# Agent attention with a squared-ReLU layer on one core: TensorE matmuls split over pairs of 64-row tiles

## The chip, the core and the metric

One core of one Trainium2 chip. The metric is the device time in microseconds from the start to the end of one execution. Five engines work side by side and meet at semaphores: TensorE (PE: matmuls and weight loads), VectorE (DVE), ScalarE (ACT), GpSimd (POOL) and SyncE (SP, which issues the DMAs). TensorE writes its results to PSUM, eight banks of 512 fp32 columns on 128 partitions; ACT and DVE read them there.

## The reference

Agent attention over 4 batches of 12480 tokens with 128 channels and 49 agents, and behind it a two-layer network of width 2048 with relu(h)² between its layers, on all 49920 tokens:

```python
s1 = scale * (agents @ k.T);  a2k = softmax(s1);  agent_v = a2k @ v     # 49 x 128
s2 = scale * (q @ agents.T);  q2a = softmax(s2);  x = q2a @ agent_v     # tokens x 128
h = x @ w_in;  r = maximum(h, 0);  g = r * r;  out = g @ w_out          # 128 -> 2048 -> 128
```

All in fp32. The softmax adds 1e-9 to its sum.

## The kernel before, in words

**Folding.** `x @ w_in` is `q2a @ (agent_v @ w_in)`, so for each batch the kernel makes W = agent_v @ w_in (49 x 2048) and multiplies the 49 probabilities of a token straight into it. Where two operands go into a matmul each is split in a high part, rounded to fp32r, and the low rest, and three products are summed: high·high, high·low, low·high.

**Blocks.** The tokens go in 52 groups s of 960 (ST), two halves of 480 columns (TT) side by side in two PSUM banks. The 2048 hidden units go in 16 pieces of 128. A block i = 16 s + j is one group and one hidden piece; there are 832 of them, and each goes through this chain:

- `mm1` (L371): h = the three products of W and the probabilities, into a pair of banks. It is called for two blocks at once. The 49 high rows, the 49 low rows and 28 of the 49 rows of the third product are stacked on 126 partitions, so that one matmul of 126 rows (L381, tiles w_a and p_a) does most of it; the other 21 rows sit in four copies at partitions 0, 32, 64 and 96 (w_b, p_b), and four matmuls of 21 rows, one for each half of each of the two blocks, go into four different row groups of the array (L384).
- `relu` on ACT (L388), `square` on ACT (L392), `high` on DVE (L396, gh: the rounded part), `low` on DVE (L400, gl = g − gh).
- `mm2` (L402, matmuls at L411): out += wo_hi·gh + wo_lo·gh + wo_hi·gl, six matmuls of 128 rows and 480 columns, accumulated over the 16 blocks of a group in two banks (out0, out1); then `store` (L425) copies one half with ACT, the other with DVE, and SP writes them out.

The step numbers set the order of each engine: a list of (time, function) pairs is sorted and issued in that order. At step i stand mm1(i), mm1(i+1) and their relus (even i), square, high and low of block i, and mm2 of block i − LAG, with LAG = 4. In this order low(i) stands directly behind high(i) on DVE, and needs its result.

**Attention beside it.** `plan_tokens` places for each later group: `q_scores` (L318: eight fp32 matmuls, which the trace shows as 16 passes, 49 columns moving and 120 columns of weights), a softmax over DVE, ACT and POOL, the split into high and low, eight transposes (L355), copies into p_a, and `q_spread`, five DMAs that put the rows at their partitions. `plan_batch` places for each next batch 13 tiles of keys (`k_scores`, L159) in the first half of a batch's time, and 13 tiles of values (`v_acc`, L213, added up by `v_sum`, L220, on DVE) in its second half, then four `w_make` (L295 to L301), whose low rows reach w_a and w_b by DMA. `chain` gives each operation the first free step of its engine, and counts the attention's two PSUM banks (pool ps_a); `hop` says how many steps must lie between engines. PSUM holds two pairs for h, two banks for out, two for attention. The first batch's attention runs ahead of the blocks.

## Time and profile before

| | before |
|---|---|
| median of 3 runs | 2051.46 us (2050.95 to 2055.99) |
| span of the profiled execution (its own time is given by this span alone) | 2049.0 us |
| what the median has above that span | 2.5 us |
| PE busy, weight loads busy | 2023.5 us, 1585.0 us |
| DVE, ACT, POOL busy | 1832.5, 1728.7, 245.7 us |
| granted TensorE clock, mean | 0.995 |

The span runs from the first to the last instruction of the execution. PE and PEld are the matmuls and the weight loads of TensorE, which run beside each other. A matmul's end is modelled, so its duration (about 380 ns for 480 columns) is longer than the time from its start to the next one's start, and this second time is what a matmul costs in a row of them. In a timeline, equal instructions that follow on one another are drawn together, with their count behind the x; square brackets give idle time of the engine and what ended it. Names are those of the program: p_a is the tile of probabilities, w_a and w_b those of W, gh and gl the two parts of g, ps_att a bank of the attention.

### The profile page before, as it was taken

The numbers are of one execution on the slowest core, as the hardware profiler recorded it, in microseconds if no ns is written. First come the engines' busy times: TensorE is split into PE (matmuls) and PEld (weight loads), VectorE is DVE, ScalarE is ACT, GpSimd is POOL, SyncE is SP. The second block draws the span as 40 slices with busy tenths as digits, with TensorE's granted clock in tenths as the row PEclk, the third lists the DMA queues.
The fourth block names the chain that finished last, engine by engine and source line by source line (L and its number), as shares of the span: only waits on it lengthen the run. The fifth ranks groups of instructions, "written<-read, shape, count | busy, mean of one in ns | idle before, by whom it ended". The sixth has DMA issues, their size and how long they took to land.

```text
span 2049.0 us, 30335 instructions
## 1 busy us (share of the span) xinstructions
PE 2023.5 (99%) x11015; PEld 1585.0 (77%) x11019; DVE 1832.5 (89%) x2282; ACT 1728.7 (84%) x2167; POOL 245.7 (12%) x206
## 2 busy tenths in 40 slices
PE   8899999999999999999999999999999999999999
PEld 7677877777778877777777887777777777777777
DVE  6778889999888889999998888999998898989898
ACT  2478789899888888999888888999888888989897
POOL 2100012221000001232100000122210000000000
PEclk9899999999999999999999999999999999999999
DMA  9322122221111122122112121122111111001110
GB/s 294 105 64 69 55 63 69 67 60 40 54 66 60 58 70 69 53 75 59 35 46 78 51 77 59 54 74 69 44 35 51 44 31 45 30 27 44 31 35 25
DMA packets 44425, 124.75 MB, mean 61 GB/s; under 512 B 6292, under 2 KB 15780, under 8 KB 44276
## 3 DMA queue, kind: packets, MB, share of 16 engines
q1 hardware_dynamic: 44178, 122.78, 19.8%
q8 instruction: 86, 1.41, 0.3%
q14 instruction: 63, 0.52, 0.1%
q10 hardware_dynamic: 98, 0.04, 0.0%
HBM read 80.97 MB, written 25.56 MB: 52 GB/s over the span
## 4 chain that ended last, share of the span: by engine, by line
PE 81%; DVE 11%; issue 6%; ACT 2%; DMA 0%; SPq 0%; POOL 0%; DVEq 0%; ACTq 0%
PE out L411 48%; PE h L381 15%; PE h L384 7%; DVE gh L396 4%; PE ps_att L159 3%; PE ps_att L318 3%; DVE gl L400 2%; DVE vs L206 1%; PE ps_att L355 1%; PE ps_att L213 1%; PE out L231 1%; PE ps_att L295 1%; ACT g L392 1%; ACT r L388 0%; PE h L159 0%
## 5 line engine op out<-in xcount | busy, mean ns | idle before, releaser
L400 DVE TENSOR_TENSOR gl<-g,gh 128x960 fp32r<-128x960 f32 x832 | 1015.5, 1221 | 30.6
L388 ACT ACTIVATE r<-h 128x960 f32<-128x960 f32 x832 | 764.0, 974 | 181.1 <-PE h L384 178.3
L392 ACT ACTIVATE g<-r 128x960 f32<-128x960 f32 x832 | 825.7, 1016 | 5.8 <-DVE gl L400 5.8
L411 PE MATMUL out<-gh,wo_hi 128*128 128x480 f32 x1664 | 688.9, 414 | 6.9 <-DVE ob L429 4.1
L396 DVE CAST gh<-g 128x960 fp32r<-128x960 f32 x832 | 585.2, 703 | 92.1 <-ACT g L392 88.7
L411 PE MATMUL out<-gl,wo_hi 128*128 128x480 f32 x1664 | 634.1, 381 | 1.7 <-DVE gl L400 1.2
L411 PE MATMUL out<-gh,wo_lo 128*128 128x480 f32 x1664 | 515.0, 380 | 1.1 <-POOL wo_lo L120 1.1
L381 PE MATMUL h<-p_a,w_a 126*128 126x480 f32 x1664 | 435.8, 383 | 5.5 <-DMA w_a<-w_lo 3.8
L411 PEld LDWEIGHTS out<-gh,wo_hi 128*128 128x128 f32 x1664 | 313.0, 188 | 141.8 <-issue 72.8
L381 PEld LDWEIGHTS h<-p_a,w_a 126*128 126x128 f32 x1664 | 309.9, 189 | 56.0 <-issue 5.6
L411 PEld LDWEIGHTS out<-gh,wo_lo 128*128 128x128 f32 x1664 | 312.9, 188 | 49.2 <-POOL wo_lo L120 1.5
L411 PEld LDWEIGHTS out<-gl,wo_hi 128*128 128x128 f32 x1664 | 314.4, 189 | 42.0 <-DVE gl L400 6.1
L341 POOL TENSOR_TENSOR e<-e,sm 120x392 f32<-120x392 f32 x52 | 55.3, 1063 | 1261.3 <-DVE sm L338 1136.7
L384 PE MATMUL h<-p_b,w_b 21*128 21x480 f32 x1664 | 204.4, 479 | 0.0
L384 PEld LDWEIGHTS h<-p_b,w_b 21*128 21x128 f32 x1664 | 80.2, 181 | 139.4 <-issue 138.5
L318 PEld LDWEIGHTS ps_att<-ag_sb,qt 128*120 128x120 f32 x832 | 96.8, 187 | 3.9 <-issue 0.4
L318 PE MATMUL ps_att<-ag_sb,qt 128*120 128x49 f32 x832 | 94.3, 267 | 0.0
L195 POOL TENSOR_TENSOR pe<-sk,pe 120x392 fp32r<-120x392 f32 x39 | 53.3, 1366 | 234.7 <-ACT pe L192 192.6
L159 PEld LDWEIGHTS ps_att<-ag_sb,kt 128*120 128x120 f32 x688 | 78.6, 185 | 3.0 <-issue 0.5
L159 PE MATMUL ps_att<-ag_sb,kt 128*120 128x49 f32 x688 | 76.7, 264 | 0.1
L348 POOL TENSOR_TENSOR pp<-e,pp 120x392 fp32r<-120x392 f32 x52 | 56.9, 1095 | 156.7 <-ACT pp L345 156.7
L163 ACT COPY sk<-ps_att 120x392 f32<-120x392 f32 x43 | 20.9, 487 | 59.7 <-PE ps_att L159 59.7
(107 smaller groups left out, 966.6 us busy)
## 6 DMA issues: line engine op xcount, KB each, us to landing
kt<-kT SPq DMA_DIRECT2D x52, 480.0 KB
vt<-v SPq DMA_DIRECT2D x52, 480.0 KB
qt<-qT SPq DMA_DIRECT2D x52, 480.0 KB
outT<-ob SPq DMA_DIRECT2D x51, 480.0 KB
p_b<-p_a SPq DMA_DIRECT2D x208, 39.4 KB
p_a<-p_a SPq DMA_DIRECT2D x52, 105.0 KB
raw<-w_in SPq DMA_DIRECT2D x4, 512.0 KB
raw<-w_out SPq DMA_DIRECT2D x4, 512.0 KB
```

What stands on the lines that cost most here:

```text
L159: nc.tensor.matmul(ps[:CH, c * A:(c + 1) * A], kt[:, c, :], ag_sb[:, b, :], start=True, stop=True)
L195: eng.tensor_tensor(out=pes[n][:, :, A:], in0=piece(n), in1=pes[n][:, :, :A].bitcast(F32), op=ALU.subtract)
L318: nc.tensor.matmul(ps[:CH, c * A:(c + 1) * A], qt[:, c * CH:(c + 1) * CH], ag_sb[:, s // NS, :], start=True, stop=True)
L341: eng.tensor_tensor(out=es[s], in0=es[s], in1=sms.pop(s).to_broadcast([CH, G, A]), op=ALU.mult)
L348: eng.tensor_tensor(out=pps[s][:, :, A:], in0=es.pop(s), in1=pps[s][:, :, :A].bitcast(F32), op=ALU.subtract)
L381: nc.tensor.matmul(hs[x][:, t, :TT], wa[:K, (x % NF) * P:(x % NF + 1) * P], pa[:K, t, :], start=True, stop=False)
L384: nc.tensor.matmul(hs[i + r // 2][:, r % 2, :TT], wb[rows, i % NF // 2, :], pb[rows], start=False, stop=True)
L388: nc.scalar.activation(rs_[i], hs.pop(i)[:, :, :TT], AF.Relu)
L392: nc.scalar.activation(gs[i], rs_.pop(i), AF.Square)
L396: nc.vector.tensor_copy(ghs[i], gs[i])
L400: nc.vector.tensor_tensor(out=gls[i], in0=gs.pop(i), in1=ghs[i].bitcast(F32), op=ALU.subtract)
L411: nc.tensor.matmul(o[t][:, :TT], w[:, j, :], x[:, t, :], start=st, stop=sp)
```

## The change

**TensorE.** Nearly all matmuls of the loop are cut into two of 64 partitions (LOW, 0 to 63, and HIGH, 64 to 127), issued in turn, one on each half of the array's rows, each writing its own PSUM bank. `mm1` is called for one block at a time and does three products for each of the two column halves: half 0 on the low tile, half 1 on the high tile, 49 rows each, six matmuls. The four 21-row matmuls are gone. `mm2` has 12 matmuls of 64 rows: in its first half (x = 0) the low tile sums into one output bank and the high tile into the other, in its second half (x = 1) they change banks. Scores, value sums and transposes are cut in the same way. `w_make` (128 rows), and the transposes of `k_max` and `a_final`, stay on the whole array; W's low rows are now written straight from PSUM into w_b by DVE, without a DMA, and `q_spread` has two DMAs where it had five.

**Banks that change tiles.** Before a bank is written by the other tile, `pass_on` puts a `nop` on GpSimd that depends on the last matmul of the first half, and `take_over` makes the first matmul of the second half depend on that nop. Between the two halves of mm2 stands `mm1` of block i. In the block behind the end of a group (`late`), mm1 comes first, and the second half of the next group's scores (`q_half(s, 1)`) stands between.

**ACT and DVE.** square(i) is placed at step i + 1.2, high(i) at i + 1.35, low(i) at i + 2.4; output is five blocks behind (LAG 5). `v_sum` adds two banks where it added one. Two tiles of keys are scored as a pair and copied and reduced by one operation each. The attention has one pair of banks.

On PE, in the middle of the loop. Before, one call of mm1 for two blocks (L381, L384) and mm2 of one block (L411); out_8198 and out_8199 are the two output banks:

```order
L381 MATMUL h<-p_a,w_a 128x480 [waits Activation_49]
L381 MATMUL h<-p_a,w_a 128x480
L381 MATMUL h<-p_a,w_a 128x480 [waits Activation_49]
L381 MATMUL h<-p_a,w_a 128x480
L384 MATMUL h<-p_b,w_b 128x480 x4
L411 MATMUL out_8198<-gh,wo_hi 128x480 [waits DVE_49]
L411 MATMUL out_8198<-gl,wo_hi 128x480 [waits DVE_49]
L411 MATMUL out_8199<-gh,wo_hi 128x480
L411 MATMUL out_8199<-gl,wo_hi 128x480
L411 MATMUL out_8198<-gh,wo_lo 128x480
L411 MATMUL out_8199<-gh,wo_lo 128x480
```

After, the first half of mm2 (L492), mm1 of one block (L464), and the start of mm2's second half:

```order
L492 MATMUL out_6581<-gh,wo_hi 128x480
L492 MATMUL out_6582<-gh,wo_hi 128x480
L492 MATMUL out_6581<-gh,wo_lo 128x480
L492 MATMUL out_6582<-gh,wo_lo 128x480
L492 MATMUL out_6581<-gl,wo_hi 128x480 [waits DVE_49]
L492 MATMUL out_6582<-gl,wo_hi 128x480
L464 MATMUL h<-p_a,w_a 128x480 [waits Activation_49]
L464 MATMUL h<-p_a,w_a 128x480
L464 MATMUL h<-p_b,w_a 128x480 x2
L464 MATMUL h<-p_a,w_b 128x480 x2
L492 MATMUL out_6582<-gh,wo_hi 128x480 [waits Pool_sequencer_49]
L492 MATMUL out_6581<-gh,wo_hi 128x480
```

A block had 2 matmuls of L381, two of L384 and six of L411; it has 6 of L464 and 12 of L492, and the two output banks change places behind mm1.

On DVE, in the middle of the loop; the numbers tell the buffers apart. Before, each gl takes the gh made just ahead of it:

```order
L396 CAST gh_5527<-g_5525 128x960
L400 TENSOR_TENSOR gl_5535<-g_5525,gh_5527 128x960
L396 CAST gh_5540<-g_5538 128x960
L400 TENSOR_TENSOR gl_5542<-g_5538,gh_5540 128x960
L396 CAST gh_5566<-g_5564 128x960
```

After:

```order
L476 CAST gh_7210<-g_7208 128x960
L480 TENSOR_TENSOR gl_7212<-g_7175,gh_7177 128x960
L476 CAST gh_7238<-g_7236 128x960
L480 TENSOR_TENSOR gl_7240<-g_7208,gh_7210 128x960
L476 CAST gh_7266<-g_7264 128x960
```

The two operations still alternate, but gl_7240 takes gh_7210, which was made two instructions earlier.

The diff, cut to its core:

```diff
+    def pass_on(key, mm):
+        relays[key] = nc.gpsimd.nop()
+        tc.add_manual_dep(relays[key].ins, mm.ins.name, SYNC, reason="bank changes row tile")
+
+    def take_over(key, mm):
+        if key in relays:
+            tc.add_manual_dep(mm.ins, relays.pop(key).ins.name, SYNC, reason="bank changes row tile")
...
     def v_acc(n):
...
         for c in range(G):
-            nc.tensor.matmul(pss["v", n][:A2, :VW], pe[:, c, :], vs[:, c], start=c == 0, stop=c == G - 1)
+            for t, rows in enumerate((LOW, slice(64, CH))):
+                nc.tensor.matmul(ps[:A2, t, :VW], pe[rows, c, :], vs[rows, c], start=c == 0, stop=c == G - 1)
...
     def q_spread(s):
         pa, pb = PT[s]
-        nc.sync.dma_start(out=pa[A2:K].bitcast(F32), in_=pa[:X].bitcast(F32))
-        for r in range(4):
-            nc.sync.dma_start(out=pb[32 * r:32 * r + R].bitcast(F32), in_=pa[X:A, r % 2].bitcast(F32))
+        nc.sync.dma_start(out=pb[:A].bitcast(F32), in_=pa[64:M, 0].bitcast(F32))
+        nc.sync.dma_start(out=pb[64:M].bitcast(F32), in_=pa[:A, 1].bitcast(F32))
...
     def mm1(i):
...
-        for x in (i, i + 1):
-            hs[x] = ps_h.tile([P, 2, 512], F32, name="h")
+        hs[i] = new_h()
+        for n in range(3):
             for t in range(2):
-                nc.tensor.matmul(hs[x][:, t, :TT], wa[:K, (x % NF) * P:(x % NF + 1) * P], pa[:K, t, :], start=True, stop=False)
-        for r in range(4):
-            rows = slice(32 * r, 32 * r + R)
-            nc.tensor.matmul(hs[i + r // 2][:, r % 2, :TT], wb[rows, i % NF // 2, :], pb[rows], start=False, stop=True)
+                rows = slice(64 * t, 64 * t + A)
+                w, p = (wb if n == 2 else wa)[rows, f], pb[rows] if n == 1 else pa[rows, t, :]
+                nc.tensor.matmul(hs[i][:, t, :TT], w, p, start=n == 0, stop=n == 2)
...
+    def mm2(i, x):
...
+        for n, (w, g) in enumerate(((wo_hi, gh), (wo_lo, gh), (wo_hi, gl))):
+            for t, rows in enumerate((LOW, HIGH)):
+                u = t ^ x ^ (j % 2)
+                mm = nc.tensor.matmul(o[u][:, :TT], w[rows, j, :], g[rows, u, :], start=j == 0 and x == 0 and n == 0, stop=j == NF - 1 and x == 1 and n == 2)
+                take_over(("o", i), mm)
+        if x == 0:
+            pass_on(("o", i), mm)
...
-    LAG = 4
+    LAG = 5
...
-    hop = {"PE": {"PE": 1, "ACT": 0, "DVE": 0}, "ACT": {"PE": 2, "ACT": 1, "DVE": 0, "POOL": 0, "SP": 0},
+    hop = {"PE": {"PE": 1, "ACT": 0, "DVE": 0}, "ACT": {"PE": 2, "ACT": 1, "DVE": 0, "POOL": 3},
...
     for i in range(NG + LAG):
+        j, late = i - LAG, i < LAG or (i - LAG) % NF == 0
         if i < NG:
-            if i % 2 == 0:
-                at(i, mm1, i)
-                at(i + .1, relu, i)
-                at(i + .12, relu, i + 1)
-            at(i + .55, square, i)
-            at(i + .6, high, i)
-            at(i + (.65 if i % 2 else 1.25), low, i)
+            at(i if late else i + .01, mm1, i)
+            at(i + .1, relu, i)
+            at(i + 1.2, square, i)
+            at(i + 1.35, high, i)
+            at(i + 2.4, low, i)
...
+        if j >= 0:
+            at(i + (.01 if late else 0), mm2, j, 0)
+            at(i + .03, mm2, j, 1)
```

More of the change, by code (lines that the diff above doesn't have):

```diff
@@ L290, in w_make @@
         if f == 0 and step == 0:
-            W[b] = (wk.tile([P, F], F32R, name="w_a"), wk.tile([P, NF // 2, P], F32R, name="w_b"))
+            W[b] = (wk.tile([P, F], F32R, name="w_a"), wk.tile([P, F], F32R, name="w_b"))
         wa, wb = W[b]
@@ L350, in q_transpose @@
     def q_transpose(s):
-        PT[s] = (wk.tile([P, 2, TT], F32R, name="p_a"), wk.tile([P, TT], F32R, name="p_b"))
-        for half in range(2):
-            ps = pss["t", s, half] = bank()
-            for c in range(H):
-                nc.tensor.matmul(ps[:A2, c * CH:(c + 1) * CH], pps[s][:, half * H + c, :], ident_r[:CH, :CH], start=True, stop=True)
-    def q_copy(s, half):
-        nc.scalar.copy(PT[s][0][:A2, half, :], pss.pop(("t", s, half))[:A2, :TT])
+        ps = pss["t", s] = new_h() if many[0] else att()
@@ new lines, in q_transpose, with q_copy @@
+        for c in range(G):
+            for t, rows in enumerate((LOW, slice(64, CH))):
+                n = rows.stop - rows.start
+                nc.tensor.matmul(ps[:M, t, c * n:(c + 1) * n], pps[s % 2][rows, c, :], ident_r[rows, rows], start=True, stop=True)
+    def q_copy(s):
+        PT[s] = (wk.tile([P, 2, TT], F32R, name="p_a"), wk.tile([P, TT], F32R, name="p_b"))
+        ps = pss.pop(("t", s))
+        to = PT[s][0][:M].rearrange("p t (c n) -> p (t c) n", n=CH)
+        nc.scalar.copy(to[:, :, :64], ps[:M, 0, :].rearrange("p (c n) -> p c n", n=64))
+        nc.scalar.copy(to[:, :, 64:], ps[:M, 1, :G * (CH - 64)].rearrange("p (c n) -> p c n", n=CH - 64))
@@ L470, in chain @@
                 held = range(ts[0], ts[-1] + 2) if todo[0][0] == "PE" else ()
-                if all(banks.get(y, 0) + need <= 2 for y in held):
+                if not any(y in banks for y in held):
                     break
                 t += 1
-            for y in held:
-                banks[y] = banks.get(y, 0) + need
+            banks.update(held)
             for (e, f, *args), g in zip(todo, ts):
@@ L481, in chain, with plan_queries, plan_queries_early, plan_turns @@
         return first, t
-    reads_bank = (k_copy, k_pmax, k_max, v_sum, a_final, w_make, q_max, q_sub, q_copy)
-    def plan_tokens(s, base, loaded=False):
-        first, end = chain(base, [("PE", q_scores, s), ("DVE", q_max, s), ("DVE", q_sub, s), ("ACT", q_exp, s), ("DVE", q_sum, s), ("DVE", q_inverse, s),
-                                ("POOL", q_norm, s), ("ACT", q_hi, s), ("POOL", q_lo, s),
-                                ("PE", q_transpose, s), ("ACT", q_copy, s, 0), ("ACT", q_copy, s, 1)])
+    reads_bank = (kp_copy, kp_max, k_max, v_sum, a_final, w_make, q_shift, q_copy)
+    def plan_queries(s):
+        t = (s - 3) * NF + NF - 1 + LAG
+        g = t + 1
+        while ("DVE", g) in taken:
+            g += 1
+        banks.update(range(t, g + 2))
+        taken.add(("DVE", g))
+        at(t - 6, q_load, s)
+        at(t + .5, q_half, s, 0)
+        at(t + 1.02, q_half, s, 1)
+        at(g + .5, q_shift, s)
+        _, ends[s] = chain(g + 1, [("ACT", q_exp, s), ("DVE", q_total, s), ("POOL", q_norm, s), ("ACT", q_hi, s), ("POOL", q_lo, s)])
+    def plan_queries_early(s, base, loaded):
+        first, ends[s] = chain(base, [("PE", q_half, s, 0), ("PE", q_half, s, 1), ("DVE", q_shift, s), ("ACT", q_exp, s), ("DVE", q_total, s),
+                                      ("POOL", q_norm, s), ("ACT", q_hi, s), ("POOL", q_lo, s)])
         if not loaded:
             at(first - 6, q_load, s)
+    ends = {}
+    def plan_turns(s):
+        _, end = chain(max(ends[s] + 1, (s - 1) * NF), [("PE", q_transpose, s), ("ACT", q_copy, s)])
         at(end + .9, q_spread, s)
@@ L607, in agent_attention_relu2_kernel @@
     at(3.95, warm_up, 2)
-    plan_tokens(1, 1, True)
+    plan_queries_early(1, 0, True)
+    plan_turns(1)
     for f in range(2, F // 512):
-        _, e = chain(4 * f - 7, [("PE", w_make, 0, f, 0), ("ACT", w_make, 0, f, 1), ("DVE", w_make, 0, f, 2)])
-        at(e + .9, w_make, 0, f, 3)
-    chain(8, [("DVE", wo_make, 3, x) for x in range(7)] + [("ACT", wo_split, 3, 0), ("POOL", wo_split, 3, 1)])
+        chain(4 * f - 7, [("PE", w_make, 0, f, 0), ("ACT", w_make, 0, f, 1), ("DVE", w_make, 0, f, 2)])
+    _, end = chain(8, [("DVE", wo_make, 3, x) for x in range(7)] + [("ACT", wo_split, 3, 0)])
+    at(end + .6, wo_split, 3, 1)
+    assert end < 3 * PW // P + LAG
+    plan_queries_early(2, 9, False)
+    for s in range(3, NSG):
+        plan_queries(s)
     for s in range(2, NSG):
-        plan_tokens(s, (s - 1) * NF)
+        plan_turns(s)
     for b in range(1, B):
```

197 lines of the change are left out of this document (120 added, 77 removed).

## The prediction

> **What bounds the kernel now.** I read the page's busy times first, then the same by stage, then the chain of work that ended last in one stretch of the loop, then single instructions there.
>
> ```profile
> PE 2023.5 (99%) x11015; PEld 1585.0 (77%) x11019; DVE 1832.5 (89%) x2282; ACT 1728.7 (84%) x2167; POOL 245.7 (12%) x206
> PE 81%; DVE 11%; issue 6%; ACT 2%; DMA 0%; SPq 0%; POOL 0%; DVEq 0%; ACTq 0%
> ...
> 300.00:500.00 200.00, 197.29 (x1061) 153.60 (x1061) 196.79 (x236) 184.54 (x246) 49.72 (x37) 1.00 0.21 59
> 500.00:820.00 320.00, 320.00 (x1762) 251.79 (x1760) 276.68 (x347) 269.66 (x331) 21.63 (x19) 1.00 0.20 61
> ```
>
> The columns of the last two rows are window, length, then PE, PEld, DVE, ACT, POOL, clock. TensorE is the bound; at 500 to 820 us it has no gap and DVE has 14% to spare. At 300 to 500 us, where a batch's values are summed (two more stages are like it, 820 to 1000 and 1300 to 1500, 580 us together), DVE is as full as PE, at 98.4%. The clock is full, so PE's time is a count of instructions. The chain shows what one pair of blocks costs:
>
> ```profile
> 613.89 0.86 PE h L381 x4
> 614.76 0.42 PE h L384 x4
> 615.17 2.81 PE out L411 x12
> 617.98 1.62 PE ps_att L159 x16
> ```
>
> Two blocks take 0.86 + 0.42 + 2.81 = 4.09 us; a score tile pushed in takes 1.62. Inside this (timeline of PE and its weight loads; start, duration):
>
> ```profile
> 599.68 0.38 PE L381 MATMUL h<-p_a,w_a 126*128 126x480 f32 x1
> 599.99 0.19 PEld L384 LDWEIGHTS h<-p_b,w_b 21*128 21x128 f32 x4 [0.34 <-issue]
> 599.99 0.49 PE L384 MATMUL h<-p_b,w_b 21*128 21x480 f32 x4
> 600.41 0.19 PEld L411 LDWEIGHTS out<-gh,wo_hi 128*128 128x128 f32 x1 [0.22 <-issue]
> 600.41 0.48 PE L411 MATMUL out<-gh,wo_hi 128*128 128x480 f32 x1
> 600.52 0.19 PEld L411 LDWEIGHTS out<-gl,wo_hi 128*128 128x128 f32 x1
> 600.73 0.37 PE L411 MATMUL out<-gl,wo_hi 128*128 128x480 f32 x1
> 600.73 0.19 PEld L411 LDWEIGHTS out<-gh,wo_hi 128*128 128x128 f32 x1
> 600.94 0.38 PE L411 MATMUL out<-gh,wo_hi 128*128 128x480 f32 x1
> 601.17 0.38 PE L411 MATMUL out<-gl,wo_hi 128*128 128x480 f32 x1
> ```
>
> From start to start a matmul of 480 columns costs .73, .94, .17: 0.21 to 0.23, and L381 0.86/4 = 0.215. I take a slot of 0.2175 us. The next load runs in that time (600.73, beside the matmul of 600.73). At L384 this stops: it starts 0.31 after the matmul ahead of it, the next matmul 0.42 later, and the second after it 0.32 later, 1.05 us for what would be three slots (0.65). Changing from 128-row matmuls to 21-row ones and back costs 0.40 us for each two blocks. The four loads of L384, on four row groups, lie inside 0.19 us, the length of one: separate row groups load and multiply at the same time.
>
> **The change, part by part.**
>
> *The blocks on PE.* A block gets 3 + 6 = 9 pairs of 64-row matmuls, all in one form of the array, so the 0.40 goes; a pair counts as one slot, because row groups run side by side. Two blocks: 18 x 0.2175 = 3.915 us against 4.09, a saving of 0.175; times 416: **−73 us**. The slot of a pair is the one price the trace doesn't show. Below: the four L384 matmuls took 0.42, less one load of 0.11 (600.41 to 600.52) and less the 0.11 by which such a change outlasts a 0.20 stream (0.31 at 599.68), so a stream alone is 0.20. Above: if the two loads of a pair are taken one behind the other, 0.11 + 0.11 = 0.22; if a load isn't hidden at all, 0.20 + 0.11 = 0.31. I take the middle, 0.2175, because the loads in order and the whole array give nearly the same; each 0.001 us of slot is 7488 x 0.001 = 7.5 us of span.
>
> [...]
>
> *The attention on PE.* Rows of the chain:
>
> ```profile
> 306.02 0.67 PE ps_att L355 x8
> ...
> 330.42 0.96 PE ps_att L213 x8
> ```
>
> Transposes: eight pairs with weights of 113 columns where 98 took 0.67, so 0.77: +0.10 x 52 = **+5**. Scores: as many passes on each tile as before, loads side by side: 1.62 stays, but two halves have a boundary more, about 0.1 x 70 = **+7**. Value sums: between nothing (0.96 stays) and loads one behind the other (0.67/8 = 0.084 each, 16 x 0.084 = 1.34): 0 to 15 us over 39 tiles; I take **+5**. The matmuls left on the whole array, six a batch (four of w_make, one transpose each of k_max and a_final), in three batches, now each change the array's form and back: 18 x 0.40 = **+7**.
>
> Each score tile has twice as many instructions, 32 matmul passes. [...] No row here shows a long run of pairs; the shortest sustained step is the 0.084 above.
>
> *The hand-over by GpSimd.* A matmul's modelled end is 0.38 after its start. How long engines take to hear of each other:
>
> ```profile
> 601.83 1.78 PE L159 MATMUL ps_att<-ag_sb,kt 128*120 128x49 f32 x16
> 603.64 0.49 ACT L163 COPY sk<-ps_att 120x392 f32<-120x392 f32 x1 [1.24 <-PE ps_att L159]
> ...
> 562.87 0.20 DVE L338 RECIPROCAL sm<-sm 120x8 f32<-120x8 f32 x1
> 563.21 1.09 POOL L341 TENSOR_TENSOR e<-e,sm 120x392 f32<-120x392 f32 x1 [33.40 <-DVE sm L338]
> ```
>
> PE to ACT 0.03 (603.61 to 603.64), DVE to POOL 0.14. With T the start of the last matmul in mm2's first half, the second half may start its load at T + 4 x 0.2175 − 0.11 = T + 0.76 without loss. The relay needs 0.38 and two hand-overs of 0.03 to 0.14: T + 0.44 to T + 0.66. I take **0**; mm1's three pairs hide it. Without them, up to 0.66 − 0.11 = 0.55 us a block would show. What is queued behind a waiting nop is POOL's normalising, subtracting and splitting; what is queued ahead of it must not wait: each such operation is now placed three steps behind its producer, so it starts right behind a nop and has a block's time, 1.96 us, for its 1.1 to 1.6. Behind PE's wait lie the rest of mm2 and the next block.
>
> *DVE and ACT.* On DVE, start and duration:
>
> ```profile
> 347.11 1.16 DVE L400 TENSOR_TENSOR gl<-g,gh 128x960 fp32r<-128x960 f32 x1
> 348.19 0.65 DVE L396 CAST gh<-g 128x960 fp32r<-128x960 f32 x1
> 348.87 1.16 DVE L400 TENSOR_TENSOR gl<-g,gh 128x960 fp32r<-128x960 f32 x1
> ...
> L220 DVE TENSOR_TENSOR acc<-ps_att,acc 98x258 f32<-98x258 f32 x36 | 15.0, 418 | 0.0
> ```
>
> gl, which needs gh, starts 0.03 behind its end; gh, which needs nothing of gl, starts 0.08 before gl's end. With both independent DVE saves 0.11 a block, some 9 us of a 200 us stage (85 blocks); the second operation of v_sum gives back 13 x 0.34 = 4.4. So DVE needs 197 − 5 = 192 us where PE will need about 200 − 42 x 0.175 = 193. DVE's saving is no gain of its own: it makes room for PE's. The gaps of PE in those stages (2.7 of 200 us) should shrink: **−5**. ACT has more room (184.5 of 200) and keeps it. One new order costs nothing: the copies of a finished group have mm1 (0.65) and half a score tile (0.8) as cover before the next group writes the banks; the row of the copy, 0.65 us on DVE, fits.
>
> *Start and end.* The DMA of W's low rows goes from the path (PE waited for it once, row below): **−4**. One block more of lag: **+2**. The three DMAs fewer in each spread free SP only; DMA engines are idle enough.
>
> ```profile
> PE h L381 <- DMA w_a<-w_lo: 3.8, 1, 3.8
> ```
>
> Sum: −73 + 5 + 7 + 5 + 7 − 5 − 4 + 2 = −56. The profiled span is 2049.0, so 1993, and the median lies 2.5 above the span: **1995 us**. With slots of 0.2135 to 0.222 this case alone spans 1965 to 2030.
>
> **The rivals.**
>
> *Pairs stream without the gap.* The slot is 0.20 to 0.205: two tiles out of step hide each other's change of weights. For it: the 0.20 of L384; against: nothing shows a second round on a tile. Two blocks take 3.6, saving 0.49 x 416 = 204; but in the 580 us of value stages DVE allows only 5 of 200, about 15 there, plus PE's 143 in the other 36.5 of 52 groups, less 17 of the attention and start terms: 2049 − 158 + 17 = 1908; DVE's own slack could carry some 10 more. **1900.**
>
> *Pairs are slower than a whole matmul.* Break-even is at a slot of (4.09 − 17/416)/18 = 0.225 (17 is the sum of the small terms above). At 0.235, if a second load waits for the other tile's start: 18 x 0.235 − 4.09 = 0.14 x 416 = 58, plus 17: **2127 us**. Against it: four tiles started together at 599.99.
>
> *The relay is late (slower).* Place: the first matmul of mm2's second half. Price: if GpSimd's two hand-overs and its nop take 0.53 instead of at most 0.28, the wait is 0.15 in each of 780 blocks: +117, **2112 us**. It decides from a wait of 0.07 on (56/780). For it: GpSimd shows the longest hand-over, and the nop has no row yet. Against: 0.10 to 0.32 of room.
>
> [...]
>
> *Score tiles load one tile behind the other.* 3.24 instead of 1.62: +1.62 x 88 = 143 on the forecast, **2138 us**. The four loads inside 0.19 speak against it.
>
> **How the numbers follow.** About 0.3% is what a measurement of this kernel tells from no change. Forecast 0.54 (0.03 of it in that band), gapless pairs 0.19, slower pairs 0.10 (0.02 in the band), late relay 0.09, the page's rule 0.04, serial score loads 0.04. Faster 0.51 + 0.19 = 0.70, same 0.05, slower 0.08 + 0.09 + 0.04 + 0.04 = 0.25. The likeliest, 1995, is the prediction. For 8 in 10 the range takes the forecast's own, gapless pairs down to 1900, and the milder half of the slow cases, up to 2075; left out are the full prices of the late relay, slow pairs and both load cases.
>
> **What would show it.** Right: matmuls of L464 and L492 in pairs that start within hundredths of a microsecond or half a slot apart, 0.2175 from pair to pair; no gap ahead of mm1; gh and gl overlapping by 0.08 on DVE; POOL's relay leaving PE no wait. Wrong: a wait of PE for POOL in each block; a chain that runs through DVE or ACT for more than the value stages; a score half over 1 us; pairs at another slot, which moves the result by 7.5 us for each nanosecond.

## The result, and the profile after

The changed kernel takes **2079.24 us** (median of 6 runs, 2064.29 to 2082.51); the kernel before, on the same chip, 2055.87 us (2050.95 to 2056.50). The ratio is 1.0107 with a 95% interval of 1.0076 to 1.0137: about 1% slower, where I forecast 1995 us. The profiled execution of the changed kernel took 2064.29 us, with a span of 2062.2; the others had spans of 2068 to 2080, and the longer, the lower their mean granted clock (0.990 in the profiled one, 0.979 in the longest).

Page and windows of the changed kernel (same rows as were shown of before; windows: PE, PEld, DVE, ACT, POOL, clock):

```profile
PE 2006.6 (97%) x19795; PEld 1827.2 (89%) x19795; DVE 1780.3 (86%) x2303; ACT 1762.0 (85%) x2202; POOL 318.1 (15%) x261
PE 70%; DVE 13%; ACT 11%; issue 5%; POOL 1%; ACTq 0%; DVEq 0%; POOLq 0%
...
300.00:500.00 200.00, 190.77 (x1878) 169.37 (x1876) 184.19 (x239) 177.23 (x235) 56.77 (x38) 0.99 0.17 50
500.00:820.00 320.00, 317.95 (x3271) 295.88 (x3267) 270.55 (x342) 279.10 (x339) 32.55 (x30) 1.00 0.17 55
```

TensorE has less to do (2023.5 before, 2006.6 now) and waits more: 9 of 200 us in the value stage, and 2 of 320 in the quiet one, where it had no gap. VectorE, full before in the value stage, now has 16 of 200 us to spare, and yet the chain goes through it and ScalarE for 24%. Nobody is full, and everybody waits.

The mechanism on TensorE came out as forecast. Timeline of the changed kernel, mm1 of one block (L464):

```profile
635.13 0.38 PE L464 MATMUL h<-p_a,w_a 49*128 49x480 f32 x1
635.13 0.19 PEld L464 LDWEIGHTS h<-p_b,w_a 49*128 49x128 f32 x1
635.35 0.38 PE L464 MATMUL h<-p_b,w_a 49*128 49x480 f32 x1
635.42 0.38 PE L464 MATMUL h<-p_a,w_a 49*128 49x480 f32 x1
635.57 0.37 PE L464 MATMUL h<-p_a,w_b 49*128 49x480 f32 x1
635.64 0.38 PE L464 MATMUL h<-p_b,w_a 49*128 49x480 f32 x1
```

One tile's matmuls start at .13, .35, .57, the other's at .42, .64: 0.22 us from one to the next on a tile, two tiles at once, and the next load of a tile starts beside that tile's running matmul (635.13). That is the 0.2175 of the forecast.

What I had missed stands at the end of a group. Timeline of the changed kernel:

```profile
638.80 1.15 DVE L480 TENSOR_TENSOR gl<-g,gh 128x960 fp32r<-128x960 f32 x1
...
639.87 0.65 DVE L507 COPY ob<-out 128x480 f32<-128x480 f32 x1
...
640.58 0.18 PEld L492 LDWEIGHTS out<-gh,wo_hi 64*128 64x128 f32 x1 [0.63 <-DVE ob L507]
```

The last matmul of the group started at 638.48, so VectorE's copy of the finished bank could have begun near 638.9. It stood behind a gl that had begun at 638.80, ran from 639.87, and the next group's mm2 waited 0.63 us for it. The waits of weight loads for that copy, of before and of the changed kernel (total us, times, longest):

```profile
PEld out L411 <- DVE ob L429: 10.9, 15, 1.0
```

```profile
PEld out L492 <- DVE ob L507: 35.8, 51, 1.7
```

For the stages I count groups by ScalarE's copy of a finished group. Its starts at both ends of the second value stage, in the kernel before, in the changed one, and in experiment e4 below:

```profile
752.98 0.56 ACT L428 COPY ob<-out 128x480 f32<-128x480 f32 x1
983.00 0.54 ACT L428 COPY ob<-out 128x480 f32<-128x480 f32 x1
```

```profile
752.49 0.55 ACT L503 COPY ob<-out 128x480 f32<-128x480 f32 x1
992.90 0.56 ACT L503 COPY ob<-out 128x480 f32<-128x480 f32 x1
```

```profile
749.13 0.55 ACT L503 COPY ob<-out 128x480 f32<-128x480 f32 x1
985.50 0.60 ACT L503 COPY ob<-out 128x480 f32<-128x480 f32 x1
```

Six groups take 983.00 − 752.98 = 230.0 us, 992.90 − 752.49 = 240.4, and 985.50 − 749.13 = 236.4. Worked out in the same way (value stages: six groups; quiet group: mean of eight in the last batch):

| kernel | value stages 1, 2, 3 | quiet group |
|---|---|---|
| before | 229.8, 230.0, 229.8 | 35.18 |
| changed | 244.1, 240.4, 241.1 | 34.43 |
| e4, copy first | 240.6, 236.4, 237.1 | 33.98 |
| e8, before with gl set apart | 238.4, 238.4, 238.2 | 36.10 |
| e11, copy first, gl adjacent | 253.9, 248.4, 246.4 | 34.0 |
| e13, copy first, no low parts | 230.1, 228.6, 228.6 | 33.98 |
| e14, copy first, one sum | 236.5, 234.3, 234.4 | 34.0 |
| e16, copy first, GpSimd one step behind | 241.5, 235.7, 235.7 | 35.4 |
| e17, copy first, gap in each block | 241.7, 236.0, 236.4 | 34.1 |
| e18, copy first, gap in each third block | 240.2, 233.9, 234.3 | 34.0 |

So the loss has two places: 0.45 us at the end of each group, and 10 to 14 us in each value stage, where the forecast had a gain.

### The profile page after: what moved, and what is told of

It is laid out like the page before. It is cut to its first block, busy times and chain, and to the rows that moved or that the text cites. A ratio compares the mean times of both kernels' runs of the same rounds, so it can differ in the third digit from the quotient of the medians.

```text
span 2062.2 us, 47894 instructions
## 1 busy us (share of the span) xinstructions
PE 2006.6 (97%) x19795; PEld 1827.2 (89%) x19795; DVE 1780.3 (86%) x2303; ACT 1762.0 (85%) x2202; POOL 318.1 (15%) x261
## 4 chain that ended last, share of the span: by engine, by line
PE 70%; DVE 13%; ACT 11%; issue 5%; POOL 1%; ACTq 0%; DVEq 0%; POOLq 0%
PE out L492 40%; PE h L464 19%; DVE gl L480 7%; PE ps_att L194 5%; ACT r L468 5%; ACT g L472 5%; DVE gh L476 2%; PE ps_att L433 2%; DVE ob L507 1%; DVE vs L265 1%; PE ps_att L273 1%; PE out L292 1%; PE ps_att L353 1%; POOL pp L422 1%; PE out L624 0%
## 5 line engine op out<-in xcount | busy, mean ns | idle before, releaser
L492 PE MATMUL out<-gh,wo_hi 64*128 64x480 f32 x3328 | 892.6, 390 | 23.3 <-DVE ob L507 15.5
L492 PE MATMUL out<-gl,wo_hi 64*128 64x480 f32 x3328 | 863.0, 381 | 8.7 <-DVE gl L480 8.4
L492 PE MATMUL out<-gh,wo_lo 64*128 64x480 f32 x3328 | 867.1, 380 | 0.9 <-POOL wo_lo L121 0.9
L492 PEld LDWEIGHTS out<-gh,wo_hi 64*128 64x128 f32 x3328 | 511.4, 186 | 76.4 <-DVE ob L507 35.8
L492 PEld LDWEIGHTS out<-gl,wo_hi 64*128 64x128 f32 x3328 | 504.8, 185 | 46.9 <-DVE gl L480 22.9
L492 PEld LDWEIGHTS out<-gh,wo_lo 64*128 64x128 f32 x3328 | 512.9, 187 | 19.1 <-POOL wo_lo L121 1.3
L464 PE MATMUL h<-p_a,w_a 49*128 49x480 f32 x1664 | 430.5, 387 | 0.0
L464 PE MATMUL h<-p_b,w_a 49*128 49x480 f32 x1664 | 424.9, 379 | 0.0
L464 PE MATMUL h<-p_a,w_b 49*128 49x480 f32 x1664 | 423.8, 378 | 0.0
L464 PEld LDWEIGHTS h<-p_a,w_b 49*128 49x128 f32 x1664 | 250.9, 186 | 17.1
L464 PEld LDWEIGHTS h<-p_b,w_a 49*128 49x128 f32 x1664 | 253.3, 189 | 11.4
L464 PEld LDWEIGHTS h<-p_a,w_a 49*128 49x128 f32 x1664 | 250.3, 186 | 11.2 <-ACT wo_hi L119 0.8
L194 PEld LDWEIGHTS ps_att<-ag_sb,qt 64*120 64x120 f32 x1632 | 119.7, 185 | 6.3 <-DVE acc L281 2.4
L194 PE MATMUL ps_att<-ag_sb,qt 64*120 64x49 f32 x1632 | 114.1, 261 | 2.0 <-DVE acc L281 1.6
L194 PEld LDWEIGHTS ps_att<-ag_sb,kt 64*120 64x120 f32 x1152 | 74.7, 181 | 0.9
```

Source lines behind the costliest of these rows:

```text
L194: mm = nc.tensor.matmul(ps[:CH, u, r * A:(r + 1) * A], cols[u][r][rows], ag_sb[rows, b, :], start=x == 0 and r == 0, stop=x == 1 and r == ...
L464: nc.tensor.matmul(hs[i][:, t, :TT], w, p, start=n == 0, stop=n == 2)
L492: mm = nc.tensor.matmul(o[u][:, :TT], w[rows, j, :], g[rows, u, :], start=j == 0 and x == 0 and n == 0, stop=j == NF - 1 and x == 1 and n ...
```

## The experiments

The theories were: **A**, VectorE's lead is bounded by gh's four buffers; **B**, VectorE without gaps starves GpSimd, whose late results stall TensorE; **C**, the copy at a group's end stands behind a gl; **D**, a stall halves TensorE's clock for a while and so grows; later **L** (lead), **V** (VectorE's own load) and **R** (the relay). All ratios are to the kernel before on the same chip.

| run | us | ratio, 95% interval |
|---|---|---|
| e1 adjacent | 2138.74 | 1.0419 (1.0402 to 1.0437) |
| e2 five gh | 2069.14 | 1.0089 (1.0072 to 1.0107) |
| e3 lag 4 | 2313.69 | 1.1271 (1.1253 to 1.1288) |
| e4 copy first | 2037.92 | 0.9928 (0.9915 to 0.9941) |
| e5 copy first, lag 6 | 2144.06 | 1.0460 (1.0430 to 1.0490) |
| e6 copy first, gl adjacent in each fourth block | 2123.67 | 1.0342 (1.0299 to 1.0384) |
| e7 copy first, no relay | 2066.98 | 1.0079 (1.0051 to 1.0106) |
| e8 before, gl set apart | 2102.63 | 1.0253 (1.0226 to 1.0281) |
| e9 copy first, five gh | 2035.85 | 0.9915 (0.9893 to 0.9936) |
| e10 copy first, margin | 2057.88 | 1.0020 (1.0004 to 1.0035) |
| e11 copy first, adjacent | 2083.23 | 1.0143 (1.0121 to 1.0164) |
| e12 copy first, five gh, margin | 2057.98 | 1.0017 (1.0003 to 1.0031) |
| e13 copy first, no low parts | 2012.20 | 0.9797 (0.9772 to 0.9822) |
| e14 copy first, one sum | 2028.44 | 0.9878 (0.9857 to 0.9899) |
| e15 copy first, stalls by hand | 2059.14 | 1.0030 (1.0016 to 1.0044) |
| e16 copy first, GpSimd one step behind | 2071.81 | 1.0092 (1.0070 to 1.0114) |
| e17 copy first, gap in each block | 2037.81 | 0.9921 (0.9901 to 0.9941) |
| e18 copy first, gap in each third | 2030.06 | 0.9879 (0.9854 to 0.9903) |

### The copy at a group's end: e4, e8

```diff
-            at(i + 2.4, low, i)
+            at(i + (3.3 if (i + 3 - LAG) % NF == NF - 1 else 2.4), low, i)
```

> The changed kernel with VectorE's copy of a finished group put ahead of the one gl that stood ahead of it in VectorE's queue. Theory C: the wait of about 0.5 us at the end of each of 52 groups goes, 52 x 0.5 = 26 us, in part given back where VectorE has no idle time: 2053 to 2067 us; the waits of the first matmul of mm2 for the copy shrink from 51 us in all to under 25. Theories A and B: a gl more than a microsecond later is made up or not, 2075 to 2085.

Measured 2037.92: the change in ratio is 1.0107 − 0.9928 = 1.79%, 37 us, more than C's 26, and the version beats the kernel before. Between the two profiled executions, whose clocks are nearly the same (0.990 and 0.988), the spans differ by 25.3 us, which is C's price; the other five executions of the changed kernel ran at 0.979 to 0.988, those of e4 at 0.988 to 0.992, so that I put the remaining 12 down to the clock. The waits for the copy all but went:

```profile
PEld out L492 <- DVE ob L507: 2.3, 5, 0.6
```

A quiet group now takes 33.98 us, 1.20 less than before. By my terms, 16 blocks x 0.0875 = 1.4, less 0.1 for the transposes and 0.1 for the scores' second half, is 1.2. So the mechanism of the pairs was worth what I said, and in the changed kernel more than a third of it (0.45 of 1.20) was lost to one instruction that stood one place too far ahead.

The same part alone in the kernel before:

```diff
-            at(i + (.65 if i % 2 else 1.25), low, i)
+            at(i + 1.62, low, i)
```

> The kernel before with gl one block behind its gh on VectorE, and nothing else of the change. My reasons on record: VectorE saves 0.11 us a block, which is room only; TensorE's gaps of some 8 us in the value stages shrink: 2041 to 2051 us against 2051. Theory B: VectorE without gaps starves GpSimd here too, whose results TensorE needs: 2055 to 2080, with GpSimd operations of over 5 us where the longest was 1.9. Since setting apart is worth 60 us in the changed kernel (2139 without it), a third case is that it is worth as much here: 2000 or less.

Measured 2102.63, 52 us slower; all three expectations missed. GpSimd's operations had no part in it (the longest 2.6 us). A quiet group became 0.92 us longer (35.18 to 36.10), and the wait is the same one:

```profile
PEld out L411 <- DVE ob L429: 51.8, 48, 1.4
```

These waits grew by 41 us, and those for gl, which is now a block later with LAG still at 4, from 19.4 to 31.7. So "dependent operations set apart", one of the parts of the change, costs a group's end some 0.8 us by itself, in a kernel without pairs.

### Order and distance: e1, e11, e3, e5, e6, e2, e9

e1 and e11 put gl right behind its gh again, without and with the copy first:

```diff
-            at(i + 2.4, low, i)
+            at(i + 1.4, low, i)
```

> The changed kernel with gl right behind its gh on VectorE again; everything else of the change stays. Theory A (lost slack): set apart, gl(i+3) stands behind gh(i+4) in VectorE's queue, and gh(i+4) waits for a buffer until the second half of mm2(i) is done; with gl next to gh one gl more (1.18 us) is ready at that moment. In the three value stages the changed kernel loses about 80 us of TensorE's time where the kernel before lost about 16, so 40 to 60 us come back: 2020 to 2040 us against 2079. Theory B (GpSimd starved): only the long GpSimd operations (7.8 to 11.6 us in the changed kernel, at most 1.9 before) go, with the few waits that they cause: 10 to 25 us, 2054 to 2069. Theory C (the copy at a group's end): no change, 2079. My reasons on record: VectorE needs 0.11 us a block more, and in the value stages the time rises by some 10 us.

> The changed kernel with the copy first and gl right behind its gh in every block: what setting apart is worth by itself when the copy at a group's end costs nothing. If its worth is VectorE's time (0.11 us a block, which counts in the value stages alone, about 250 blocks of 832), 28 us: 2060 to 2075 us. If the loss of 60 us against the changed kernel stays whole, 2090 to 2105. If GpSimd's starving outweighs it, under 2038.

Measured 2138.74 and 2083.23. Theory A said that this would win 40 to 60 us; it lost 60, and 45 with the copy first. A is wrong, and so was "room only" in my prediction: setting apart is worth 45 us in this kernel, 35 of them in the six-group stages of the table and nearly all of the rest in the groups right behind them. A part of it is that gl right behind its gh now starts 0.10 us behind gh's end (in e11, gh from 324.31 for 0.65 us, gl at 325.07), where it was 0.03 in the kernel before; so each block costs VectorE 0.19 us more than set apart, and not 0.11. What it does is shown by e11's timeline of VectorE and of a score tile's loads:

```profile
331.17 1.16 DVE L480 TENSOR_TENSOR gl<-g,gh 128x960 fp32r<-128x960 f32 x1
332.25 0.42 DVE L280 TENSOR_TENSOR acc<-ps_att,acc 98x258 f32<-98x258 f32 x1
332.70 0.43 DVE L281 TENSOR_TENSOR acc<-ps_att,acc 98x258 f32<-98x258 f32 x1
...
333.18 0.92 PEld L194 LDWEIGHTS ps_att<-ag_sb,qt 64*120 64x120 f32 x16 [2.75 <-DVE acc L281]
```

TensorE had finished the value sums at 326.9, but VectorE came to them at 332.25, behind three pairs of gh and gl. There is only one two-bank tile for all the attention, so the next score tile waited 2.75 us. Eleven such waits make 23.8 us, four more of the transposes 14.4. Much of the price comes by way of the clock: in the three stages it stood at one half for 27.3, 27.3 and 20.5 us in e11, and for 6.8, 3.4 and 6.8 in e4. At a loss of about half of such time (a slot took 0.40 us there in e15, against 0.22), this alone is some 29 of the 45 us (an estimate; how waits and half clock hang together is seen with e15 below).

The distance between mm1 and mm2 (`LAG = 5` to 4 in e3; to 6 in e5, with the copy first):

> The changed kernel with the output four blocks behind instead of five; gl stays set apart. Theory A: gh(i+4) waits for mm2(i) whatever the distance to mm1, so nothing comes back, and ScalarE has a block less of lead: 2079 to 2100 us. A rival, that the longer distance itself took the slack: 2030 to 2060. Theories B and C: 2079.

> The changed kernel with VectorE's copy of a finished group first (as in e4_copy_first, 2038 us) and the output six blocks behind instead of five. What is left of the loss is in the three value stages, where TensorE waits 14 times a stage for gl, some 24 us in all. Theory L (lead): four blocks cost 235 us against five, so the path from mm1 over ScalarE and VectorE to mm2 is still short of time at five where the attention's work stands between; with six 10 to 30 us come back: 2008 to 2028. Theory B (GpSimd starved by a VectorE without gaps) and theory R (the relay's nop stands behind long GpSimd operations): no change or worse, 2035 to 2050.

Measured 2313.69 and 2144.06; both theories missed by far. With four blocks TensorE waits for gl in more than half of its 832 blocks:

```profile
PEld out L492 <- DVE gl L480: 395.4, 478, 1.8
```

So five blocks are a must here with gl set apart. With six, the wait for gl is no longer among the greatest, but waits for GpSimd's pe and pp (30.0 and 13.9 us) and for ScalarE's copy (23.2) are. More distance doesn't mean more slack here: the planner's table puts the attention's steps elsewhere with it.

gl adjacent in each fourth block only:

```diff
-            at(i + (3.3 if (i + 3 - LAG) % NF == NF - 1 else 2.4), low, i)
+            at(i + (1.36 if i % 4 == 0 else 3.3 if (i + 3 - LAG) % NF == NF - 1 else 2.4), low, i)
```

> The changed kernel with the copy first and, in every fourth block, gl right behind its gh, so that VectorE has a short gap about every 8 us. Theory B: no GpSimd operation lasts over about 8 us and most stay under 2, the waits of TensorE for pp (2.6 us, twice), for the relay (9.8 us in all) and the slow clock behind them go: 2013 to 2028 us. Theory L: VectorE works 0.03 us a block more, 2036 to 2050. With gl next to gh in every block it was 2139 without the copy first, so that a part of that loss may come too: up to 2065.

Measured 2123.67, a miss: each quiet group took 1.8 us more, since two gl then follow each other and the second, of the block before, is late for its mm2 (146 waits, 109.1 us in all). It says nothing on B.

Five buffers for gh (e2; e9 with the copy first):

> The changed kernel with five buffers for gh instead of four (the identity matrix and a row of maxima share other tiles, to make room); gl stays set apart. Theory A: gh(i+5) waits for mm2(i) where gh(i+4) did, so that one gl more is ready, as with gl next to gh, and VectorE's short gaps stay away: 2015 to 2040 us. Theory B: VectorE runs without gaps as before, GpSimd's operations still last up to 10 us in places: 2065 to 2085. Theory C: 2079.

> The changed kernel with the copy first (2038 us) and five buffers for gh. Theory A (VectorE's lead is bounded by gh's four buffers): with the copy out of the way the value stages, where TensorE waits for gl 24 us in all, get a block more of lead: 2013 to 2030 us. Rival: as without the copy first (2069 against some 2074), no effect: 2033 to 2043. Theory B (GpSimd's late results): a VectorE that is held up less leaves fewer gaps, 2038 to 2070.

Measured 2069.14 (ratio 1.0089, the changed kernel's 1.0107 inside noise) and 2035.85 (0.9915 against 0.9928): no effect either time. A is out.

### GpSimd: e7, e16, e10, e12, e13, e17, e18

What had led me to theory B, in the timeline of the changed kernel: one GpSimd operation of 196 elements a row, the first and the last of the VectorE operations beside it, and TensorE's loads behind it.

```profile
967.50 11.56 POOL L422 TENSOR_TENSOR pp<-e,pp 120x196 fp32r<-120x196 f32 x1 [2.91 <-PE out L492]
...
967.48 0.65 DVE L476 CAST gh<-g 128x960 fp32r<-128x960 f32 x1
...
977.45 1.15 DVE L480 TENSOR_TENSOR gl<-g,gh 128x960 fp32r<-128x960 f32 x1
...
979.10 1.08 PEld L433 LDWEIGHTS ps_att<-ident_r,pp 64*113 64x113 f32 x14 [2.57 <-POOL pp L422]
```

Of the 52 operations of its line the shortest took 0.61 us and the middle one 0.98. This one lasted 11.56, as long as fourteen VectorE operations followed each other without a gap. With gl next to gh (e1), where gaps of 0.10 us come between them, the longest of these operations took 1.6 us. From these two numbers I read that GpSimd's operation is held up while VectorE leaves no gap; by what means, no trace shows.

The relay taken out (both passes of a block on the same bank and row tile):

```diff
-                u = t ^ x ^ (j % 2)
+                u = t
-                take_over(("o", i), mm)
-        if x == 0:
-            pass_on(("o", i), mm)
```

> The changed kernel with the copy first and without the change of tiles in mm2: both passes of a block write the same half of the columns from the same row tile, with no nop on GpSimd between them, so that the output's halves hold one row tile's products twice. It prices the relay. My reasons on record: the relay costs nothing, 2033 to 2041 us. Theory R: the 13 late relays (9.8 us) and the slow clock behind them go, 2015 to 2028. The rival on record (a wait in each block of 0.15): 1920.

Measured 2066.98: 29 us slower than with the relay, which no theory expected. The quiet groups didn't become shorter (34.38 us against 33.98; why they are 0.4 longer is open), so the relay itself is free, as predicted. But GpSimd's work fell beside other VectorE operations, by my reading because the nops no longer tie it to TensorE's pace: sixteen of its operations lasted over 2 us instead of ten, six of them over 11 instead of two, and TensorE waited for it:

```profile
PEld ps_att L273 <- POOL pe L254: 24.0, 4, 6.0
```

The planner's distance to GpSimd, three blocks to one:

```diff
-"ACT": {..., "POOL": 3}, "DVE": {..., "POOL": 3}
+"ACT": {..., "POOL": 1}, "DVE": {..., "POOL": 1}
```

> The changed kernel with the copy first and GpSimd's operations one block behind their producers in the planner's table, as in the kernel before, instead of three. My reasons on record: three are needed so that nothing waits ahead of a nop; with one the relay is late behind GpSimd's waiting operations: 2045 to 2080 us. Theory B: starving depends on which VectorE operations lie beside GpSimd's, so that it can go either way by 20 us: 2018 to 2060.

Measured 2071.81, as my reasons on record had it. The relay is late behind GpSimd's waiting operations, once in each group:

```profile
PEld out L492 <- POOLq L165: 47.2, 52, 2.0
```

More room behind GpSimd (transposes three blocks later, value sums two), alone and with five gh:

```diff
-chain(max(ends[s] + 1, ...), [("PE", q_transpose, s), ...
+chain(max(ends[s] + (4 if s > 2 else 1), ...), [("PE", q_transpose, s), ...
-chain(max(t1 + 1, t2 + 2), [("PE", v_acc, n), ...
+chain(max(t1 + 3, t2 + 2), [("PE", v_acc, n), ...
```

> The changed kernel with the copy first, and with TensorE's use of what GpSimd makes put later: the transposes three blocks and the value sums two blocks further behind GpSimd's last operation. No operation is taken out and VectorE's queue stays as it is but for the sums. Theory B: GpSimd's operations may still last 8 to 11 us, but the waits of TensorE for pp and for the late relays behind it, and the half clock that follows them, shrink: 2013 to 2030 us. Theory A: 2033 to 2043.

> The changed kernel with the copy first, five buffers for gh and the margin behind GpSimd together, as a version that might beat the kernel before by more than the copy alone (2038 us). If both help: 2000 to 2020. If only one does: 2013 to 2030. If neither: 2033 to 2045.

Measured 2057.88 and 2057.98: 20 us worse, where B expected a gain. But later sums move every later step, and new long GpSimd operations appear (ten of over 6 us, up to 10.2, in e10; three in e4), so that these two runs don't test B alone.

GpSimd's subtractions taken out:

```diff
-        eng.tensor_tensor(out=pes[n][:, :, A:], in0=piece(n), in1=..., op=ALU.subtract)
+        eng.memset(pes[n][:, :, A:].bitcast(F32), 0.0)
-        eng.tensor_tensor(out=pp[:, :H, 64:], ...)
-        eng.tensor_tensor(out=pp[:, H:, :A], ...)
```

> The changed kernel with the copy first and without GpSimd's subtractions of the low parts: k_lo only writes zeros, q_lo is left out, so that the attention's weights are rounded. TensorE, ScalarE and VectorE do the same work as in e4_copy_first. Theory B (what GpSimd brings late, and what it does to VectorE beside it): the value stages take 223 to 230 us for six groups instead of 236 to 241, and the whole 1998 to 2020 us. Theory V (VectorE's own load): they stay, 2030 to 2040.

Measured 2012.20, 26 us less, and the value stages fell by 8 to 10 us each, to about what they were before the change. So these operations carry over half of what is left. But do they do it by starving? Two last runs keep all work and its order, and only make a gh wait for the end of the gl ahead of it on the same engine (`last["gl"]` is the gl issued last):

```diff
+        op = nc.vector.tensor_copy(ghs[i], gs[i])
+        if "gl" in last and i % 1 == 0:
+            tc.add_manual_dep(op.ins, last["gl"].ins.name, SYNC, reason="gap for GpSimd")
```

(`i % 3` in e18.)

> The changed kernel with the copy first, and each gh made to wait for the end of the gl ahead of it on VectorE: order and work as in e4_copy_first (2038 us), with a gap of some 0.03 us where the two overlapped by 0.08. Theory B (VectorE without gaps starves GpSimd, whose late results stall TensorE): no GpSimd operation over 3 us, value stages of 229 to 234 us for six groups, 2012 to 2028 us in all. Theory V (VectorE's time): 0.11 us a block more, 9 us in each value stage in which VectorE is full: 2040 to 2065. In the quiet groups nothing changes (34.0 us).

> The same with a gap in each third block only. Theory B: GpSimd's operations are held for at most three blocks, some 6 us, and the worst stalls go: 2015 to 2033 us. Theory V: a third of the cost, 2038 to 2047.

Measured 2037.81 and 2030.06. The starving is gone: all 52 operations of that line, shortest, median and longest in ns, in e4 and in e17:

```profile
L422 POOL TENSOR_TENSOR pp<-e,pp x52: 608/1012/11560, 53.5 to 1951.7; 120x196 fp32r<-120x196 f32 x52
```

```profile
L422 POOL TENSOR_TENSOR pp<-e,pp x52: 605/1006/2166, 49.5 to 1949.8; 120x196 fp32r<-120x196 f32 x52
```

But the value stages stay at 241.7, 236.0 and 236.4. The gap that ends the starving has a price of its own: in e17 a gh starts at least 0.10 us behind the end of the gl ahead of it, where the two overlapped by 0.08. TensorE no longer waits for pp (5.1 us in all in e4), and in the second and third stage its clock stays full, but its waits for gl grow from 23.8 us to 38.0. So e17 says that ending the starving by gaps wins nothing, and e18, with a third of the gaps, that it wins 8 us (10 by the ratios); what starving costs by itself they don't tell. GpSimd's work has a price beside starving, too. The second value stage in e4, e13 and e17 (window, length, PE, PEld, DVE, ACT, POOL, clock):

```profile
749.13:985.50 236.37, 227.54 (x2302) 207.61 (x2299) 218.85 (x281) 212.61 (x282) 61.12 (x41) 0.99 0.20 58
737.22:965.86 228.64, 224.16 (x2300) 206.25 (x2298) 208.93 (x281) 211.57 (x282) 35.61 (x29) 1.00 0.21 60
745.29:981.33 236.04, 226.74 (x2302) 203.86 (x2300) 222.85 (x282) 213.21 (x281) 53.29 (x41) 1.00 0.20 58
```

VectorE does the same 281 operations in e4 and in e13, and is busy for 9.9 us less without GpSimd's subtractions beside them (11.4 and 10.4 in the other two stages): gl takes 1.17 us on the mean instead of 1.21, gh 0.68 instead of 0.73. In e17 both take as long as in e4 or longer (1.22 and 0.74). So VectorE loses some 10 us a stage to GpSimd's work, starved or not, which is about what each stage gained in e13. That the gain comes from this, and not from results that are there earlier, fits these numbers but isn't shown apart.

### VectorE's load, and the clock: e14, e15

The second operation of v_sum taken out:

```diff
-        nc.vector.tensor_tensor(acc, ps[:A2, 1, :VW], acc, op=ALU.add)
```

> The changed kernel with the copy first and without the second operation of v_sum (39 of some 0.42 us on VectorE), so that the second row tile's value sums are missing from the output. Theory V: 13 x 0.42 = 5.5 us less work in each value stage, and the wait for the sums in the same bank is shorter: 5 to 8 us less in each, 2014 to 2023 us. Theory B: no gain, 2033 to 2043, or a loss if VectorE has fewer gaps.

Measured 2028.44, 9.5 us less, where 5.5 us less work in each stage makes 16.5 in all. Each stage became 2 to 4 us shorter. VectorE's load is thus part of the bound in those stages, though its busy time there shows slack; the attention's tile also comes free 0.43 us sooner in this run, which it can't tell apart.

Stalls made by hand in quiet groups, by one to four writes on GpSimd behind the relay's nop:

```diff
+        if key[0] == "o" and key[1] >= 640 and key[1] % NF == 8:
+            for _ in range(1 + key[1] // NF % 4):
+                relays[key] = nc.gpsimd.memset(idle, 0.0)
```

> The changed kernel with the copy first, and in the last twelve groups, where nothing else waits, one hand-over each that GpSimd delays by one, two, three or four writes of 480 elements. If the clock falls after a stall (theory D), the pair slots behind the longer stalls go from 0.22 to 0.39 us for some 3 us, and a group with such a stall is longer by the stall and 1.2 to 2.5 us more; short stalls cost their own length alone. If the slow slots elsewhere have another cause, all stalls cost their own length.

Timeline of e15, the matmuls behind one stall of three writes and all three of four:

```profile
1719.61 0.49 PE L496 MATMUL out<-gh,wo_hi 64*128 64x480 f32 x2 [1.75 <-POOL idle L170]
1719.93 0.38 PE L496 MATMUL out<-gh,wo_lo 64*128 64x480 f32 x2
...
1756.12 0.49 PE L496 MATMUL out<-gh,wo_hi 64*128 64x480 f32 x2 [2.25 <-POOL idle L170]
1756.45 0.38 PE L496 MATMUL out<-gh,wo_lo 64*128 64x480 f32 x2
...
1897.88 0.49 PE L496 MATMUL out<-gh,wo_hi 64*128 64x480 f32 x2 [2.24 <-POOL idle L170]
1898.21 0.38 PE L496 MATMUL out<-gh,wo_lo 64*128 64x480 f32 x2
...
1898.88 0.60 PE L496 MATMUL out<-gh,wo_lo 64*128 64x480 f32 x2
1899.28 0.60 PE L496 MATMUL out<-gl,wo_hi 64*128 64x480 f32 x2
...
2038.45 0.51 PE L496 MATMUL out<-gh,wo_hi 64*128 64x480 f32 x2 [2.09 <-POOL idle L170]
2038.77 0.59 PE L496 MATMUL out<-gh,wo_lo 64*128 64x480 f32 x2
2039.15 0.61 PE L496 MATMUL out<-gl,wo_hi 64*128 64x480 f32 x2
```

The groups took 34.4, 34.9, 35.9 and 36.5 us in the first round, so every stall cost about its own length; in the second, 34.4, 34.9, 36.0 and 38.1. Of the three stalls of four writes, the first (2.25 us) left the clock alone, and the other two (2.24 and 2.09) brought slots of 0.40 us, from one microsecond and from 0.3 us after their end on; the second cost 1.6 us more than its length. D holds for long stalls, and in this run their place decides: in e15 and e4, as in the changed kernel and the kernel before, all changes of the granted clock lie whole multiples of 3.41 us apart, and the half clock here lasted one such stretch each time (1898.84 to 1902.25, and from 2038.78 on). Laid on the stretches, the stalls of 2.24 and 2.09 us fall whole into the one just before the half clock; the one of 2.25 lies across two, 1.60 and 0.65; those of three writes put at most 1.68 us into one. So in this run stretches with 2.09 us and more of a stall were followed by half clock, and those with 1.68 and less were not. Elsewhere less was enough: of e4's three half-clock periods in the value stages, from 290.98, 973.65 and 1471.99 on, the last two follow a stretch in which 63% was without a matmul (by the modelled ends), and the first one with 37%.

In e4's value stages the clock stood at one half for 6.8, 3.4 and 6.8 us, which at a loss of about half is some 8 us in all; in the kernel before it was full there. The spread of the changed kernel's runs fits this too: from a clock of 0.990 to one of 0.981, 0.9% of 2070 us is 19 us, and they took 15 us longer.

## Why the prediction was wrong, point by point

- *Slot of a pair, 0.2175 (−73).* Right: 0.22 in the rows, and 1.20 us a quiet group with the copy out of the way. The lower bound was no evidence, though: its 0.20 was worked out with the 0.11 by which a change "outlasts a 0.20 stream", so that it went in as it came out.
- *Relay (0).* Right, but for 13 waits of 9.8 us in all in e4. Without it nothing is gained (e7), and with one step's distance instead of three it costs a wait in each group (e16). The rival "late relay" did not come true.
- *Rivals of TensorE* (gapless; slower; loads not hidden, a slot of 0.31, the first of the two chances of 0.04; serial score loads). None came true. The passes of a score half come two every 0.105 us (L194, 638.85, 638.95, 639.06), so that the 32 of a score tile take 1.68 us where its 16 took 1.62. The load at 635.13 ran for 0.19 us inside the 0.38 of a matmul of the same rows, as the one at 600.73 had in the kernel before.
- *The copies of a finished group cost nothing.* **Failed.** I took mm1 (0.65) and half a score tile as cover for a copy of 0.65 us, and did not ask what stands ahead of that copy in VectorE's queue. Set apart, it is a gl of 1.15 us: 0.45 us for each quiet group, 25 us in all at like clock and 37 between the medians (e4). The part that I had written off as a saving caused it, as e8 shows in the kernel before.
- *VectorE's saving is room; TensorE's gaps shrink (−5).* **Failed**, and it is the greater half. I set VectorE's need (192 of 200 us) beside TensorE's (193) and took the larger. The sums were about right: e4's VectorE was busy for 247.79 of 270 us, so for some 221 of the 240.6 that six groups took, and TensorE's part, with the quiet group's gain, is 229.8 − 6 x 1.2 = 222.6. What failed is that the larger sum would be the time: three stages took 714.1 us instead of 668, with both engines at about 92%. That is 46 us, about what lies between e4's 2038 and the forecast's 1995. The gaps of TensorE, which were to shrink, grew: 27 us without a matmul in e4's three stages against 7 before, and 17 us of half clock against none. Two full engines alone don't explain it, for in the kernel before they had run at 98.6% and 98.4% together.
- *What these 46 are.* 26 go with GpSimd's subtractions (e13), beside which VectorE's operations take some 10 us longer in each stage; about 9 go with one VectorE operation in each sum (e14); the slow clock holds some 8. These overlap, so they need not add up. Buffers of gh (e2, e9) are not it. Gaps for GpSimd (e17) pay for themselves only, and later uses (e10) brought new long operations. That the attention has one tile of two banks, where it had two tiles of one, was not tested; the waits for it are 6.7 us in e4. How the rest comes about, in the ring from mm1 over ScalarE and VectorE to mm2, stays open.
- *The score halves, transposes, sums and changes of form (+24).* Not priced one by one. In the seven groups between the first two value stages, e4 gained 271.0 − 260.3 = 10.7 us, 1.5 a group, so that they cost no more than I gave them.

e18, the copy first and a gap in each third block, had the shortest median of those that compute everything: 2030.06 us, 0.9879 of the kernel before (0.9854 to 0.9903).

## What to carry to other kernels

When an operation is moved in an in-order queue, look up what then stands ahead of each short, urgent operation of that engine (the copy that frees a bank), not only what the moved one waits for. Where two engines are each to run at 98% of the same stage, the larger of the two sums is the least time that the stage can take, and not a forecast: here a step that makes one of them 3% faster gained nothing there. Price GpSimd's work as work of VectorE too, which was busy for some 10 us more in each stage here with GpSimd's subtractions beside it (e4 against e13). And count a wait of TensorE with what it may do to the clock: one of 2.24 us cost 1.6 us more than its length (e15).

## What the runs showed of the hardware that I had not expected

- A GpSimd operation took 11.56 us beside fourteen VectorE operations that overlap by 0.08 us; with a gap of at least 0.10 us in each block (e17) the longest of its line took 2.17.
- The reverse: a VectorE operation of 0.68 us (vs) took up to 1.45 beside GpSimd's in the changed kernel.
- A VectorE operation that needs the result of the one ahead of it started 0.03 us behind its end in the kernel before, and 0.10 in e11.
- In e15, waits of TensorE of 2.24 and 2.09 us that lay in one 3.41 us stretch of the clock were followed by half clock, one of 2.25 across two stretches wasn't, nor was any of the stalls of 1.75 us and less.
- Two row tiles of 64 rows stream 480 columns each in the 0.22 us that one matmul of 128 rows takes, the next weights loaded beside the running matmul of the same rows.
